# The second network's first matrix product as seven Strassen block products, with its weight blocks streamed from DRAM scratch

## The chip, the cores and the metric

The kernel runs on one core of a Trainium2 chip. The metric is the device time of one launch in microseconds; three runs of the kernel before took 911.65, 911.95 and 911.99 us, median 911.95 us.

## What is computed

Attention over a window of 128 positions, then two dense networks one behind the other, over 2304 tokens of width 512, hidden width 2048:

```python
x = attention(q, k, v)                  # (2304, 512)
h = np.maximum(x @ w_in, 0.0)
x = h * h @ w_out                       # first network, "layer 0"
h = x @ w2_in                           # (2304, 512) @ (512, 2048)
g = h * np.cos(h)
out = g @ w2_out                        # second network, "layer 1"
```

All is float32. Each matrix product is made of three: both operands are split into a high part, rounded to the multiplier's format, and the low rest; high by high, high by low and low by high are added in PSUM.

## The kernel before

**Units.** `ORDER` (lines 44 to 52) lists 144 units of work. A unit is one block of tokens and one column block f of 128 hidden columns (16 of them): `h_mms(i)` makes the hidden values (4 contraction tiles x 3 matmuls, L584 to L586, into one PSUM bank), an element-wise stage follows, and `y_mms(i)` multiplies with the second matrix into four PSUM banks that collect over all f (4 output tiles x 3 matmuls, L661 to L663). Blocks 0 to 3 have 512 tokens; block 4 has 256 and takes two f in a unit. Units 0 to 71 are layer 0 (48 to 71 alternate two units of block 3 and one of block 4), 72 to 135 layer 1 on blocks 0 to 3, and 136 to 143 layer 1 on block 4.

**Element-wise stage.** Layer 0: `relu_part` and `square_part` (relu and high part on ACT, square and low part on DVE). Layer 1: `cos_reduce` (ACT `kk`, two DVE steps, a DVE clamp, ACT abs) and `cos_apply` (ACT sine, DVE product with h, ACT high part `gh`, DVE low part `gl`). h stays in PSUM until the product.

**Order.** Per unit the loop at L825 emits `cos_apply` of the next unit, one `tick`, the h products of the unit `LA` ahead (L833: 1, later 2, then 3), the element-wise stage, another `tick`, and the two halves of `y_mms`. ACT, DVE, POOL and SP run in the order that the scheduler gives them, each strictly in turn. `tick` moves the prepared jobs by one stage: weights (`w_job`: a load of 1 MB for each f and layer, `w_top` on ACT, `w_rest` on DVE, high part on ACT, low part on DVE) and layer 1's input (`x2_job`: high part on ACT, low part on DVE). A weight of layer 1 takes the place of the layer-0 weight of the same f in SBUF and can be loaded when the last unit that reads it is done. So all sixteen f of layer 1 lie in SBUF, ready for the multiplier.

**PSUM.** Four banks collect y; four (`h_slot`) take h of layer 1 in turn.

Of the kernel before, what the change touches and what calls it, by code (L numbers as in the profile page):

```python
# [22 lines left out]
P = 128  # L23
NJ = NT // P
T = 256
# [39 lines left out]


ENGINES = {mybir.EngineType.PE, mybir.EngineType.Activation, mybir.EngineType.DVE, mybir.EngineType.Pool}


class Job:  # L70


    def __init__(self, key, load, stages, gates=None, source=None, frees=1, ready=None):
        self.key, self.load, self.stages, self.frees = key, load, stages, frees
        self.gates, self.source, self.ready = gates or {}, source, ready
        self.raw, self.at = None, 0


@with_exitstack
def attention_mlp_mlp(ctx: ExitStack, tc: tile.TileContext, kq, s0, v, w1, w2, bias, ident, out):  # L80
# [37 lines left out]

    W, A2, Y = {}, {}, {}
    QH, QL, V = {}, {}, {}  # L120
    now = {"qk": -1, "v": -1, "h": -1, "y": -1}

    queues = {"a": [], "w": []}
    inflight, finished = [], set()
# [5 lines left out]
    def top_up():  # L132
        for c in "aw":
            if c == "a" and now["qk"] < A_OPEN:
                continue
            jobs = queues[c]
            while held[c] < AHEAD[c] and loads[c] < len(jobs):
                job = jobs[loads[c]]
                if job.source is not None and job.source not in finished or job.ready and not job.ready():
                    break  # L140
                job.queue = c
                if c == "a":
                    job.raw = rp.tile([P, 512], F32, tag=c, name=f"raw_{c}{loads[c]}")
                job.load(job)
                held[c] += 1
                loads[c] += 1

    def advance(job):
        job.stages[job.at](job)
        if job.at == job.frees:  # L150
            held[job.queue] -= 1
# [6 lines left out]
    late = []  # L158

    def tick(new="aw", flush=True):  # L160
        for job in list(inflight):
            if job.at not in job.gates or job.gates[job.at]():
                if not advance(job):
                    inflight.remove(job)
        while late and flush:
            late.pop(0)()
        top_up()
        for c in new:
            if started[c] < len(queues[c]):
                job = queues[c][started[c]]  # L170
                if job.raw is not None and (0 not in job.gates or job.gates[0]()):
# [23 lines left out]

    def clear(key):
        t = cv.tile([P, 1024], F32, tag="cv", name="cv_" + "_".join(map(str, key)))
        pool.memset(t, 0.0)
        return t

    def w_top(job):

        job.t = cleared.pop(0) if cleared else clear(job.key)
        top = job.t.bitcast(F16).rearrange("p (n two) -> p n two", two=2)
        act.copy(top[:, :, 1], job.raw.bitcast(BF16).rearrange("p (n q) -> p n q", q=4)[:, :, 2])
# [12 lines left out]
    def w_split(job):  # L220
        _, layer, f = job.key
        w = W[layer, f] = wp.tile([P, 2048], F32R, tag=f"w{f}", name=f"w_{layer}_{f}")
        act.copy(w[:, 0:1024], job.t)

        def lo():
            dve.tensor_tensor(w[:, 1024:2048], job.t, w[:, 0:1024].bitcast(F32), ALU.subtract)  # L226

        late.append(lo)

    def w_job(layer, f):  # L230

        last = max((i for i, (a, _, fs, _) in enumerate(ORDER) if a == layer - 1 and f in fs), default=-1)
        seen = 4 * min(f - SEAT + 1, PLAIN - 1) + 3

        def ready():
            if layer == 0 and f >= SEAT:
                return now["qk"] >= seen and now["v"] >= START - 1
            return now["y"] >= last

        return Job(("w", layer, f), w_load(layer, f), [w_top, w_rest, w_split], frees=2, ready=ready)  # L240


# [6 lines left out]
    def x_ready(layer, b):  # L249
# [3 lines left out]
        return now["h"] >= max((i for i, unit in enumerate(ORDER) if unit[:2] in old), default=-1)  # L253

    def x2_job(b, m):
        def view(part):
            x = XS[x_slot(1, b)][part]
            return x[:, :, m, :] if b < NBK else x[:, 0, 2 * m : 2 * m + 2, :]

# [306 lines left out]
    def h_mms(i):  # L566
        layer, b, fs, n = ORDER[i]
        if layer == 1:
            for m in range(KT if b < NBK else 2):
                run_until(("x", b, m))  # L570
        for f in fs:
            run_until(("w", layer, f))
        now["h"] = i
        hpool, tag = h_slot(i)
        hb = hpool.tile([P, 2, T], F32, tag=tag, name=f"h_{i}")
        Hb[i] = hb
        for c, f in enumerate(fs):
            wh, wl = W[layer, f][:, 0:512], W[layer, f][:, 1024:1536]
            o = hb[:, c] if len(fs) == 2 else hb
            for kt in range(KT):  # L580
                cs = slice(kt * P, kt * P + P)
                xs = XS[x_slot(layer, b)]
                xh, xl = (part[:, :, kt] if n is None else part[:, n, kt] for part in xs)
                te.matmul(o, wh[:, cs], xh, start=(c == 0 and kt == 0), stop=False, skip_group_check=True)  # L584
                te.matmul(o, wh[:, cs], xl, start=False, stop=False, skip_group_check=True)  # L585
                te.matmul(o, wl[:, cs], xh, start=False, stop=(kt == KT - 1), skip_group_check=True)  # L586

# [4 lines left out]
    def square_part(i):  # L592
# [9 lines left out]
        lo = dve.tensor_tensor(rl, a, rh.bitcast(F32), ALU.subtract)  # L602
        A2[i] = (rh, rl)
        return hi, lo

# [11 lines left out]
    def cos_apply(i):  # L617
# [5 lines left out]
        dve.tensor_tensor(r, r, hb, ALU.mult)  # L623
        act.copy(rh, r)  # L624
        dve.tensor_tensor(rl, r, rh.bitcast(F32), ALU.subtract)  # L625
        A2[i] = (rh, rl)
# [6 lines left out]
    def y_mms(i, cs, ms=range(KT)):  # L633
# [11 lines left out]
        if tokens_out(layer, b):  # L645
            for t in ms if tuple(ms) != tuple(range(KT)) else range(2):
                for c in cs:
                    wh, wl = (W[layer, fs[c]][:, k : k + 512] for k in (512, 1536))
                    gh, gl = (g[:, c, t * P : t * P + P] for g in (rh, rl))
# [5 lines left out]
        for m in ms:  # L655
            o = Y[b][m // 2][:, m % 2] if two else Y[b][m] if n is None else Y[b][m][:, n]
            for c in cs:
                wh, wl = (W[layer, fs[c]][:, k + m * P : k + m * P + P] for k in (512, 1536))
                gh, gl = (rh[:, c], rl[:, c]) if per == 2 else (rh, rl)
# [10 lines left out]
    def y_out(layer, b):  # L670
        for k, yb in enumerate(Y.pop(b)):
            if gp2 is not None and k % 2:
                ysb = gp2.tile([P, 2, T], F32, tag="ysb", name=f"ysb_{layer}_{b}_{k}")
            else:
                ysb = gp.tile([P, 2, T], F32, tag="a", name=f"ysb_{layer}_{b}_{k}")
            (dve.tensor_copy if k % 2 else act.copy)(ysb, yb)  # L676
# [8 lines left out]
    def y_tail(i):  # L685

        for t in range(2):
            y_mms(i, (0, 1), (t,))
            for k, copy in enumerate((dve.tensor_copy, act.copy)):
                ypool, tag = (gp, "a") if t else (gp2, "ysb")  # L690
                ysb = ypool.tile([P, 2, T], F32, tag=tag, name=f"ysb_tail_{t}_{k}")[:, 0]
                copy(ysb, Y[NBK][t][:, k * T : k * T + T])
# [3 lines left out]


    MARKS = [(-1, START), (14, 32), (29, 50), (30, 52), (45, 66), (48, STEPS)]

# [6 lines left out]
    for j in range(PLAIN - 1, NJ):  # L706
        queues["a"] += [kq_job(j, hp) for hp in range(4)]
    queues["a"] += [x2_job(b, m) for b in range(NBK + 1) for m in range(KT if b < NBK else 2)]
    queues["w"] += [w_job(layer, f) for layer in range(2) for f in range(NF)]

    with ExitStack():
# [113 lines left out]
        for i in range(len(ORDER)):  # L825
            if s >= STEPS and gp2 is None:
# [5 lines left out]
                gp2 = ctx.enter_context(tc.tile_pool(name="gp2", bufs=2))  # L832
            LA = 1 if i < NG1 - 2 else 2 if i < NG1 else 3  # L833
# [5 lines left out]
            if i + 1 < len(ORDER) and ORDER[i + 1][0] == 1:  # L839
                cos_apply(i + 1)  # L840
            tick("aw" if s >= STEPS else "a")
            new = range(emitted, min(i + LA + 1, len(ORDER)))
            emitted = max(emitted, new.stop)
            for m in new:
# [11 lines left out]
            if i + 1 == len(ORDER):  # L856
                y_tail(i)
                break
            if len(ORDER[i][2]) == 2:
# [3 lines left out]
            y_mms(i, *halves[0])  # L863
            if todo > 0:
                values_of_block()
                s += 1
            if todo > 1:
# [3 lines left out]
                s += 1  # L871
            y_mms(i, *halves[1])
            values_of_block()

# [60 lines left out]
```

## Time and profile before

| | |
|---|---|
| runs | 911.65, 911.95, 911.99 us |
| profiled execution | 911.92 us, its span 910.1 us, granted clock 0.997 |
| PE busy | 900.4 us, 99% of the span |
| DVE, ACT, POOL busy | 582.9, 473.5, 93.1 us |
| DMA | 69.18 MB, mean 76 GB/s |

The span runs from the first to the last instruction; 1.8 us lie around it. A matmul's duration in the records overlaps the next one's, so its cost is the distance between two starts. In a timeline row the first number is the start, the second the duration, and the bracket at its end says how long the engine was idle before and what ended that.

### The profile page before, as it was taken

How to read it: one execution, taken by the hardware profiler on the slowest of the kernel's cores; microseconds unless marked ns; L12 is line 12 of the kernel's file. 1: busy time of each engine (PE TensorE's matmuls, PEld its weight loads, DVE VectorE, ACT ScalarE, POOL GpSimd, SP SyncE). 2: the span in 40 equal slices, each digit the busy share in tenths (PEclk: the TensorE clock that was granted, in tenths of full speed). 3: DMA queues.
4: the chain of work that ended last, by engine and by line, in shares of the span. 5: the costliest groups of instructions: out<-in, count | busy, mean ns of one | idle time of the engine just before them, and what ended most of it. 6: DMA issues, size and time to landing. Idle time of an engine off the chain costs nothing.

```text
span 910.1 us, 13087 instructions
## 1 busy us (share of the span) xinstructions
PE 900.4 (99%) x4898; PEld 748.2 (82%) x4898; DVE 582.9 (64%) x1343; ACT 473.5 (52%) x1018; POOL 93.1 (10%) x164
## 2 busy tenths in 40 slices
PE   9899999999999999999999999999999999999998
PEld 7677788788888888888888888888888888888897
DVE  7699676666676666745454785665566555655553
ACT  6799555454454444544454774454444444444443
POOL 3332221101111111201011000000000000000000
PEclk9999999999999999999999999999999999999999
DMA  9752032311121111242423620020001000100010
GB/s 369 284 223 94 13 127 70 102 50 59 47 90 61 59 47 47 83 139 98 179 94 125 212 103 1 13 81 1 0 1 47 1 1 0 47 1 1 1 47 23
DMA packets 25870, 69.18 MB, mean 76 GB/s; under 512 B 2640, under 2 KB 8144, under 8 KB 25808
## 3 DMA queue, kind: packets, MB, share of 16 engines
q1 hardware_dynamic: 25376, 68.16, 21.3%
q8 instruction: 38, 0.62, 0.3%
q10 hardware_dynamic: 432, 0.20, 0.1%
q14 instruction: 24, 0.20, 0.1%
HBM read 58.91 MB, written 9.44 MB: 75 GB/s over the span
## 4 chain that ended last, share of the span: by engine, by line
PE 88%; DVE 7%; ACT 3%; issue 1%; DMA 1%; POOL 0%; DVEq 0%; ACTq 0%; POOLq 0%
PE h L584 13%; PE h L585 13%; PE h L586 13%; PE y L661 13%; PE y L663 12%; PE y L662 12%; PE o L532 3%; PE s L380 2%; PE t L479 1%; DVE cv_w L211 1%; DVE w L226 1%; PE junk L114 1%; PE y L651 1%; PE y L652 1%; PE y L653 1%
## 5 line engine op out<-in xcount | busy, mean ns | idle before, releaser
L584 PE MATMUL h<-xh,w 128*128 128x512 f32 (+1 forms) x640 | 237.3, 371 | 0.0
L585 PE MATMUL h<-xl,w 128*128 128x512 f32 (+1 forms) x640 | 236.1, 369 | 0.0
L586 PE MATMUL h<-xh,w 128*128 128x512 f32 (+1 forms) x640 | 235.8, 368 | 0.0
L584 PEld LDWEIGHTS h<-xh,w 128*128 128x128 f32 x640 | 120.7, 189 | 21.0 <-issue 0.3
L586 PEld LDWEIGHTS h<-xh,w 128*128 128x128 f32 x640 | 120.6, 189 | 20.5
L585 PEld LDWEIGHTS h<-xl,w 128*128 128x128 f32 x640 | 120.8, 189 | 18.8
L661 PE MATMUL y<-rh,w 128*128 128x512 f32 (+1 forms) x320 | 123.2, 387 | 0.5 <-DVE ysb L676 0.5
L663 PE MATMUL y<-rh,w 128*128 128x512 f32 (+1 forms) x320 | 118.5, 370 | 0.0
L662 PE MATMUL y<-rl,w 128*128 128x512 f32 (+1 forms) x320 | 118.4, 370 | 0.0
L614 ACT ACTIVATE r<-r 128x512 f32<-128x512 f32 x72 | 45.5, 632 | 120.1 <-DVE r L613 120.1
L661 PE MATMUL y<-gh,w 128*128 128x512 f32 x256 | 99.6, 390 | 0.2 <-ACT gh L624 0.2
L662 PE MATMUL y<-gl,w 128*128 128x512 f32 x256 | 99.6, 389 | 0.0
L663 PE MATMUL y<-gh,w 128*128 128x512 f32 x256 | 99.6, 389 | 0.0
L625 DVE TENSOR_TENSOR gl<-r,gh 128x512 fp32r<-128x512 f32 x72 | 49.8, 691 | 74.2 <-ACT gh L624 74.1
L611 DVE SCALAR_TENSOR_TENSOR r<-kk,h 128x512 f32<-128x512 int32 x72 | 49.5, 687 | 63.9 <-ACT kk L610 63.8
L601 DVE TENSOR_TENSOR a<-a 128x512 f32<-128x512 f32 x62 | 44.3, 715 | 59.1 <-ACT rh L600 56.4
L610 ACT ACTIVATE kk<-h 128x512 int32<-128x512 f32 x72 | 43.0, 597 | 69.7 <-PE h L586 69.6
L590 ACT ACTIVATE a<-h 128x512 f32<-128x512 f32 x72 | 42.9, 596 | 69.0 <-PE h L586 67.4
L446 ACT ACTIVATE p<-s,st 128x128 f32<-128x128 f32 x112 | 40.1, 363 | 68.7 <-DVE st L430 64.3
L486 POOL TENSOR_SCALAR_AFFINE_SELECT p<-p 128x256 f32<-128x256 f32 x104 | 50.2, 483 | 246.2 <-ACT p L481 235.9
L663 PEld LDWEIGHTS y<-rh,w 128*128 128x128 f32 x320 | 60.3, 189 | 10.7
L661 PEld LDWEIGHTS y<-rh,w 128*128 128x128 f32 x320 | 60.3, 189 | 10.5 <-issue 1.7
(91 smaller groups left out, 1398.2 us busy)
## 6 DMA issues: line engine op xcount, KB each, us to landing
raw<-w_in SPq DMA_DIRECT2D x32, 1023.8 KB, 6.8
raw_a<-kq_in SPq DMA_DIRECT2D x44, 256.0 KB, 2.5
v<-v_in SPq DMA_DIRECT2D x18, 256.0 KB, 2.7
y<-ysb SPq DMA_DIRECT2D x18, 256.0 KB, 2.1
raw_a<-y SPq DMA_DIRECT2D x18, 256.0 KB, 2.8
out<-ysb SPq DMA_DIRECT2D x16, 256.0 KB, 2.3
s<-s_in SPq DMA_DIRECT2D x6, 512.0 KB, 9.4
s<-s_in SPq DMA_DIRECT2D x2, 256.0 KB, 3.2
```

Of the source, the lines that this page charges most:

```text
L486: pool.affine_select(pt[:, part], pt[:, part if quick else 0], pattern=[[0, n], [0, 2], [-sign, P]], compare_op=ALU.is_gt if part else ALU ...
L584: te.matmul(o, wh[:, cs], xh, start=(c == 0 and kt == 0), stop=False, skip_group_check=True)
L585: te.matmul(o, wh[:, cs], xl, start=False, stop=False, skip_group_check=True)
L586: te.matmul(o, wl[:, cs], xh, start=False, stop=(kt == KT - 1), skip_group_check=True)
L601: dve.tensor_tensor(a, a, a, ALU.mult)
L610: act.activation(kk, hb, AF.Copy, scale=INV2PI)
L611: dve.scalar_tensor_tensor(r, kk, -C1, hb, ALU.mult, ALU.add)
L614: act.activation(r, r, AF.Abs)
L625: dve.tensor_tensor(rl, r, rh.bitcast(F32), ALU.subtract)
L661: te.matmul(o, wh, gh, start=(first and not (two and m % 2)), stop=False, skip_group_check=True)
L662: te.matmul(o, wh, gl, start=False, stop=False, skip_group_check=True)
L663: te.matmul(o, wl, gh, start=False, stop=last, skip_group_check=True)
```

## The change

For blocks 0 to 3 of layer 1, two units (one pair u of column blocks, 256 hidden columns) become one group p = 8 b + u. Its matrix product is cut in 2 x 2 blocks of 256 and made by Winograd's form of Strassen's scheme: seven block products where the plain product has eight. `seven(p, part)` has 7 x 2 contraction tiles x 3 = 42 matmuls of 256 columns; before, two units had 24 of 512. Three products open PSUM regions d, z and e; z takes four of the seven products in turn. After each of them a copy or an addition moves what it holds to a tile of h in SBUF: per group four ACT copies and three DVE additions of 128x256. `seven` runs two groups ahead of y, in four parts, one before each half of `y_mms`. `cos_reduce` and `cos_apply` read h from SBUF.

Weights: for each u, `blocks_job` turns the first matrices of two f into the blocks A11 to A22 and their sums S1 to S4, splits these in high and low parts, and stores all eight (2 MB) in DRAM scratch `wd[u]`; `w2_job` prepares the second matrices in place. The SBUF that this frees is the arena: 20 places of 256 KB in a ring, in which `stream()` loads the seven blocks of each group (four for block 4), and tiles 0, 1 and 7 for blocks of the input. `x2_sums_job` makes the input's sums T1 to T4. A job's stage waits `LEAD` = 5 ticks behind the load; `behind()` puts these stages behind the latest element-wise operation of ACT and DVE, and stores are issued one stage after the work that fills them. `y_out` takes all its buffers from one pool of two (before: two pools).

```diff
+BLOCKS = ("A11", "A12", "A21", "A22", "S1", "S2", "S3", "S4")
+SEVEN = (("A12", "B21"), ("A11", "B11"), ("S1", "T1"), ("S2", "T2"), ("S3", "T3"), ("S4", "B22"), ("A22", "T4"))
+RING = range(2, NU - 1)
...
+    def blocks_job(u):
...
+        def sums(job):
...
+            dve.tensor_tensor(s1, a21, a22, ALU.add)
+            dve.tensor_tensor(s3, a11, a21, ALU.subtract)
+            dve.tensor_tensor(s2, s1, a11, ALU.subtract)
+            dve.tensor_tensor(s4, a12, s2, ALU.subtract)
+            hi(job, 0)
+        def middle(job):
+            lo(job, 0)
+            hi(job, 1)
+        def more(job):
+            lo(job, 1)
+            store(job, 0)
+        def end(job):
+            store(job, 1)
...
+    def stream():
+        while streamed[0] < len(groups):
...
+            if now["p"] < g - 2 or ticks[0] < landed.get(u, 1 << 30) or any(a not in Arena for a, _ in places):
+                return
+            for (a, c), name in zip(places, names):
+                Chunk[g, name] = Arena[a][:, 512 * c : 512 * c + 512]
+                sp.dma_start(Chunk[g, name].bitcast(F32), wd[u][:, BLOCKS.index(name)])
...
+    def seven(p, part):
...
+            places = ((ps_y2, "z0"), (ps_y2, "z1")) if p % 2 else ((ps_h, "h"), (ps_h2, "h"))
...
+        d, z, e = one[:, 0], one[:, 1], two[:, 0]
...
+        if part == 0:
+            product(0, d, opens=True)
+            product(1, z)
+            product(2, e, opens=True)
+            act.copy(h1[:, 0], z)
+            act.copy(h2[:, 1], e)
+            dve.tensor_tensor(h1[:, 0], h1[:, 0], d, ALU.add)
+        elif part == 1:
+            product(3, z)
+            act.copy(h1[:, 1], z)
+        elif part == 2:
+            product(4, z)
+            dve.tensor_tensor(h2[:, 1], h2[:, 1], z, ALU.add)
+        else:
+            product(5, e)
+            dve.tensor_tensor(h1[:, 1], h1[:, 1], e, ALU.add)
+            product(6, z)
+            act.copy(h2[:, 0], z)
...
+            if i >= NG1 and i < L0:
+                p, c = divmod(i - NG1, 2)
+                for q in (2 * c, 2 * c + 1):
+                    tick()
+                    if q == 0:
+                        cos_apply(i + 1)
...
+                    if p + 2 < NP:
+                        seven(p + 2, q)
...
+                    y_mms(i, (0,), (0, 1) if q % 2 == 0 else (2, 3))
...
+            if i == NG1 - 2:
+                seven(0, 0)
+                seven(0, 1)
             y_mms(i, *halves[0])
```

The instructions' order, at three places (names: h or hs hidden values in PSUM or SBUF, s the PSUM regions of a group, numbered by group; r, gh, gl by unit; the last number is a buffer's).

ACT, layer 1, before: one unit.

```order
L610 ACTIVATE kk_117_7167<-h_117_7154 128x512
L614 ACTIVATE r_117_7168<-r_117_7168 128x512
L624 CAST gh_116_7186<-r_116_7130 128x512
L622 ACTIVATE r_117_7168<-r_117_7168,halfpi_81 128x512
```

ACT, layer 1, now: one group (two units).

```order
L855 COPY hs_24_0_8302<-s_24_0_8300 128x256
L901 ACTIVATE r_118_8294<-r_118_8294 128x512
L856 COPY hs_24_1_8303<-s_24_1_8301 128x256
L909 ACTIVATE r_118_8294<-r_118_8294,halfpi_81 128x512
L901 ACTIVATE r_119_8332<-r_119_8332 128x512
L909 ACTIVATE r_119_8332<-r_119_8332,halfpi_81 128x512
L860 COPY hs_24_0_8302<-s_24_0_8300 128x256
L911 CAST gh_118_8351<-r_118_8294 128x512
L897 ACTIVATE kk_120_8403<-hs_24_0_8302 128x512
L868 COPY hs_24_1_8303<-s_24_0_8300 128x256
L897 ACTIVATE kk_121_8441<-hs_24_1_8303 128x512
L911 CAST gh_119_8397<-r_119_8332 128x512
```

The four copies stand between the steps of the units of the group before; the third (L860), which frees z for the fifth product, stands behind the sines of both units.

ACT around the start of layer 1, now (cv and hi_b belong to `blocks_job` and `w2_job` of u = 6):

```order
L283 CAST w_1_6_5649<-cv_w2_6_5605 128x1024
L855 COPY hs_1_0_5610<-s_1_0_5608 128x256
L901 ACTIVATE r_72_5554<-r_72_5554 128x512
L909 ACT_TABLE_LOAD
L909 ACTIVATE r_72_5554<-r_72_5554,halfpi_81 128x512
L901 ACTIVATE r_73_5591<-r_73_5591 128x512
L856 COPY hs_1_1_5611<-s_1_1_5609 128x256
L860 COPY hs_1_0_5610<-s_1_0_5608 128x256
L336 CAST hi_b_6_5598<-s_b_6_5633 128x1024
L911 CAST gh_72_5651<-r_72_5554 128x512
```

The copies of group 1 that free e (L856) and z (L860) now stand behind the first units' reduction and the table load.

DVE a little later, now (`cv_p` and `s_b` low parts of the blocks of u = 6, `w_1_6` of its second matrices):

```order
L912 TENSOR_TENSOR gl_72_5652<-r_72_5554,gh_72_5651 128x512
L340 TENSOR_TENSOR s_b_6_5633<-s_b_6_5633,hi_b_6_5598 128x1024
L290 TENSOR_TENSOR w_1_6_5649<-cv_w2_6_5605,w_1_6_5649 128x1024
L910 TENSOR_TENSOR r_73_5591<-r_73_5591,hs_0_1_5464 128x512
L898 SCALAR_TENSOR_TENSOR r_74_5706<-kk_74_5705,hs_1_0_5610 128x512
L857 TENSOR_TENSOR hs_2_0_5714<-hs_2_0_5714,s_2_0_5712 128x256
L912 TENSOR_TENSOR gl_73_5700<-r_73_5591,gh_73_5699 128x512
L899 SCALAR_TENSOR_TENSOR r_74_5706<-kk_74_5705,r_74_5706 128x512
L898 SCALAR_TENSOR_TENSOR r_75_5751<-kk_75_5750,hs_1_1_5611 128x512
L900 TENSOR_SCALAR r_74_5706<-r_74_5706 128x512
L899 SCALAR_TENSOR_TENSOR r_75_5751<-kk_75_5750,r_75_5751 128x512
L240 SCALAR_TENSOR_TENSOR cv_p_7_5747<-raw_b_7_5599,cv_p_7_5747 128x1024
```

Two 1024-wide low halves now stand ahead of unit 73's product (L910), and a 1024-wide step of u = 7 follows among unit 75's.

## Rows read from the trace of the kernel before

**Rows 1.** The page, part 1: busy time, share and instructions of each engine.

```profile
PE 900.4 (99%) x4898; PEld 748.2 (82%) x4898; DVE 582.9 (64%) x1343; ACT 473.5 (52%) x1018; POOL 93.1 (10%) x164
```

**Rows 2.** Windows: stretch, its length, busy time by engine, clock, DMA share, GB/s.

```profile
450.00:500.00 50.00, 50.00 (x289) 44.23 (x289) 26.37 (x30) 24.56 (x30) 5.74 (x6) 1.00 0.35 127
510.00:515.00 5.00, 5.00 (x23) 4.13 (x22) 5.00 (x9) 3.54 (x8) 0.96 (x1) 1.00 0.51 177
515.00:520.00 5.00, 4.78 (x32) 4.17 (x31) 3.97 (x7) 4.45 (x7) 0.00 (x0) 1.00 0.97 319
600.00:650.00 50.00, 50.00 (x222) 41.40 (x221) 29.35 (x48) 23.18 (x39) 0.00 (x0) 1.00 0.06 22
```

**Rows 3.** Timeline of PE: starts of 512-column, then 256-column matmuls in layer 1.

```profile
600.02 0.39 PE L661 MATMUL y<-gh,w 128*128 128x512 f32 x1
...
602.74 0.39 PE L584 MATMUL h<-xh,w 128*128 128x512 f32 x1
...
869.84 0.28 PE L584 MATMUL h<-xh,w 128*128 128x256 f32 x1
...
872.72 0.40 PE L651 MATMUL y<-w,gh 128*128 128x512 f32 x1
```

**Rows 4.** Groups by line: one matmul line at 256 columns, and its weight loads.

```profile
L584 PE MATMUL h<-xh,w 128*128 128x256 f32 x128 | 36.1, 282 | 0.0
L584 PEld LDWEIGHTS h<-xh,w 128*128 128x128 f32 x640 | 120.7, 189 | 21.0 <-issue 0.3
```

**Rows 5.** Groups of DVE by line and shape: busy us, mean ns of one, idle before.

```profile
L211 DVE SCALAR_TENSOR_TENSOR cv_w<-raw,cv_w 128x1024 int32<-128x1024 int32 x30 | 36.6, 1223 | 0.9 <-ACT cv_w L207 0.5
L611 DVE SCALAR_TENSOR_TENSOR r<-kk,h 128x512 f32<-128x512 int32 x72 | 49.5, 687 | 63.9 <-ACT kk L610 63.8
L613 DVE TENSOR_SCALAR r<-r 128x512 f32<-128x512 f32 x72 | 30.7, 426 | 2.1
L312 DVE TENSOR_TENSOR ql<-raw_a,qh 128x256 fp32r<-128x256 f32 x44 | 18.6, 423 | 1.3 <-PE s L380 1.2
```

**Rows 6.** Groups of ACT by line and shape.

```profile
L622 ACT ACTIVATE r<-r,halfpi 128x512 f32<-128x512 f32 x72 | 51.9, 721 | 0.3
L207 ACT CAST cv_w<-raw 128x1024 f16<-128x1024 bf16 x30 | 41.1, 1371 | 2.2 <-DMA raw<-w_in 1.4 <-POOL cv_w L198 0.8
L622 ACT ACT_TABLE_LOAD x1 | 1.3, 1283 | 0.0
L692 ACT COPY ysb_tail<-y 128x256 f32<-128x256 f32 x2 | 0.7, 372 | 5.1 <-DVE ysb_tail L692 5.1
```

**Rows 7.** Timeline of ACT and of DVE in one unit of layer 1.

```profile
600.22 0.60 ACT L610 ACTIVATE kk<-h 128x512 int32<-128x512 f32 x1 [1.13 <-PE h L586]
...
603.30 0.60 ACT L624 CAST gh<-r 128x512 fp32r<-128x512 f32 x1
603.81 0.72 ACT L622 ACTIVATE r<-r,halfpi 128x512 f32<-128x512 f32 x1
...
600.85 0.69 DVE L611 SCALAR_TENSOR_TENSOR r<-kk,h 128x512 f32<-128x512 int32 x1 [1.05 <-ACT kk L610]
601.58 0.69 DVE L612 SCALAR_TENSOR_TENSOR r<-kk,r 128x512 f32<-128x512 int32 x1
...
603.94 0.69 DVE L625 TENSOR_TENSOR gl<-r,gh 128x512 fp32r<-128x512 f32 x1 [1.21 <-ACT gh L624]
604.56 0.69 DVE L623 TENSOR_TENSOR r<-r,h 128x512 f32<-128x512 f32 x1
```

**Rows 8.** Timeline of PE at a pause, and the window behind it (clock before the DMA share).

```profile
32.99 0.62 PE L479 MATMUL t<-id_sb,s 128*128 128x128 f32 x3 [1.18 <-ACT s L468]
...
34.00:38.00 4.00, 4.00 (x32) 2.72 (x28) 1.20 (x3) 1.85 (x3) 2.40 (x3) 0.57 0.93 379
```

**Rows 9.** The page, part 6: DMA issues, KB each, median us from issue to landing.

```profile
raw<-w_in SPq DMA_DIRECT2D x32, 1023.8 KB, 6.8
raw_a<-y SPq DMA_DIRECT2D x18, 256.0 KB, 2.8
```

More of the change, by code (lines that the diff above doesn't have):

```diff
@@ L136, in top_up @@
             jobs = queues[c]
-            while held[c] < AHEAD[c] and loads[c] < len(jobs):
+            while loads[c] < len(jobs) and held[c] + jobs[loads[c]].raws <= AHEAD[c]:
                 job = jobs[loads[c]]
@@ L142, in top_up @@
                 if c == "a":
-                    job.raw = rp.tile([P, 512], F32, tag=c, name=f"raw_{c}{loads[c]}")
+                    raws = [rp.tile([P, 512], F32, tag=c, name=f"raw_{c}{loads[c]}_{r}") for r in range(job.raws)]
+                    job.raw = raws[0] if job.raws == 1 else raws
                 job.load(job)
-                held[c] += 1
+                job.loaded = ticks[0]
+                held[c] += job.raws
                 loads[c] += 1
+        stream()
     def advance(job):
-        job.stages[job.at](job)
+        with behind() if job.key[0] in ("p", "w2") else ExitStack():
+            job.stages[job.at](job)
         if job.at == job.frees:
-            held[job.queue] -= 1
+            held[job.queue] -= job.raws
         job.at += 1
@@ L158, in attention_mlp_mlp, with behind @@
     late = []
+    ticks = [0]
+    latest = {}
+    def behind(*engines):
+        back = ExitStack()
+        for e in engines or ("act", "dve"):
+            if e in latest:
+                back.enter_context(tc.issue_after(latest[e].ins))
+        return back
     def tick(new="aw", flush=True):
+        ticks[0] += 1
         for job in list(inflight):
@@ L170, in tick @@
                 job = queues[c][started[c]]
-                if job.raw is not None and (0 not in job.gates or job.gates[0]()):
+                if job.raw is None or job.key[0] in ("p", "w2") and ticks[0] < job.loaded + LEAD:
+                    continue
+                if 0 not in job.gates or job.gates[0]():
                     started[c] += 1
@@ L244, in attention_mlp_mlp, with run_stream @@
+    def run_stream(g):
+        for _ in range(400):
+            if streamed[0] > g:
+                return
+            tick()
+        raise RuntimeError(f"group {g}")
     XS = [[xp.tile([P, 2, KT, T], F32R, name=f"x{part}_{i}") for part in "hl"] for i in range(2)]
@@ L567, in h_mms @@
         layer, b, fs, n = ORDER[i]
+        g = NP + fs[0] // 2
         if layer == 1:
-            for m in range(KT if b < NBK else 2):
+            for m in range(2):
                 run_until(("x", b, m))
-        for f in fs:
-            run_until(("w", layer, f))
+            run_stream(g)
+            now["p"] = g
+        else:
+            for f in fs:
+                run_until(("w", layer, f))
         now["h"] = i
@@ L671, in y_out @@
         for k, yb in enumerate(Y.pop(b)):
[L672 to L675, printed above, removed]
+            ysb = gp.tile([P, 2, T], F32, tag="a", name=f"ysb_{layer}_{b}_{k}")
             (dve.tensor_copy if k % 2 else act.copy)(ysb, yb)
@@ L872, in attention_mlp_mlp @@
             y_mms(i, *halves[1])
+            if i == NG1 - 1:
+                cos_reduce(NG1 + 1)
+                for q in range(4):
+                    tick()
+                    if q == 2:
+                        cos_apply(NG1)
+                    seven(1, q)
             values_of_block()
```

259 lines of the change are left out of this document (226 added, 33 removed).

## The prediction

> **What bounds the kernel now.** The page's busy times come first: PE works 99% of the span, DVE 64%, ACT 52% [rows 1]. The windows then tell where the rest is: in the stages that the change touches PE is full in every stretch (50.00 of 50 us in layer 1) and loses 0.22 us at the one change of stage, where DVE is busy for a whole 5 us [rows 2]. So the time is PE's issue time, and what PE costs is read from distances between starts: twelve matmuls of 512 columns take 602.74 - 600.02 = 2.72 us, 226.7 ns each; twenty-four of 256 columns take 872.72 - 869.84 = 2.88 us, 120.0 ns each [rows 3]. The records of a 256-column matmul (282 ns) and of its weight load (189 ns) are longer [rows 4], but overlap.
>
> **What PE gains.** A pair of units in layer 1 has 24 h matmuls, 24 x 226.7 = 5.44 us. A group has 42 of 256 columns, 42 x 120.0 = 5.04 us. That is 0.40 us for each of 32 groups, **12.8 us**: not an eighth of the 174 us of these products, because half the columns cost 53% of the time. The Trainium skill (TensorE: Matmul & The Clock Gate, "Wait — 56ns, not 53.3ns?") gives a warm matmul its columns at 2.4 GHz and only about 2.5 ns besides; by that a group would save 24 x 215.8 - 42 x 109.2 = 593 ns, all groups 19.0 us, and the sum below would be 902.7. The rows contradict it here: both widths show some 13 ns beside their columns, so the halved width costs, and the sum goes by the rows. Layer 0 and block 4 keep their matmuls.
>
> **What a group adds beside PE.** Four copies of 128x256 on ACT (372 ns in the nearest row [rows 6]) and three additions on DVE (423 ns [rows 5]). Taken as throughput both fit: a pair of units (10.88 us) has 5.0 us of ACT and 6.4 of DVE now (23.18 and 29.35 of 50 us [rows 2]), and 1.5 and 1.3 come in, for 10.48 us. What counts is the chain, since z must be emptied before the next product may write it. I schedule one group by hand. Spacings [rows 7]: on DVE a dependent step starts 0.73 after the one it needs (601.58 - 600.85), an independent one 0.62 (604.56 - 603.94), at a record of 0.69; a hand-over to another engine takes 0.03 (600.85 - 600.22 - 0.60). So I let independent steps overlap by 0.07 to 0.09.
> Zero is a group's first product. Three products end at 2.16, half a y (6 x 226.7 = 1.36) at 3.52, S2 at 4.24, y at 5.60, S3 at 6.32, y at 7.68, S4 and A22 at 9.12, y at 10.48. S4's last result is there at 8.56; DVE's addition hands h to ACT's `kk` at 9.05; then DVE, in its order, starts the first unit's reduction 9.68, its second step 10.41, the other unit's first 11.02, the older unit's low half 11.64, a clamp 12.26, an addition 12.62, the other unit's second step 12.98, its clamp 13.71. ACT's abs follows at 14.17, the sine (721 ns [rows 6]) at 14.83, and behind it, at 15.46, the copy that frees z after S2: done 15.83. PE wants z at 10.48 + 5.60 = 16.08. **It fits by 0.25 us**, so I take 10.48 us for a group and no wait. The bounds: nothing, or, with every step at its full record (0.1 us more at six places, 0.6 in all), a wait of 0.35 us in every one of the 26 groups behind the start-up.
> At a block's end four copies of y come in. With two buffers instead of four the third waits for the first one's store, but y's banks are wanted 3.5 us or more after they close; nothing taken. The input's sums (2.2 us of ACT, 4.2 of DVE, twice per block) stand, for blocks 2 and 3, where the chain has gaps; nothing taken.
>
> **The joint stage** (units 48 to 71) has ACT and DVE half busy [rows 2]. A pair of column blocks, 16.6 us of PE, gets 1.2 us more of ACT and 2.9 of DVE (one more split and four sums), so DVE comes to about 73%. Between a unit's h and its own y lie 5.4 us of other products and the relu chain needs 2.0; the longest stretch put between (4.2 us on DVE) leaves room. Nothing; if that cover went, each wait would be 1 us or so.
>
> **The start of layer 1** is where it costs. Before, up to three units of h waited in PSUM; now groups 1 and 2 need z and e emptied while the blocks of u = 6 and 7 are still being made. Zero is the end of y of unit 68. Without waits PE would end group 0 and y of unit 70 at 16.1, y of 71 at 19.0, group 1 with two products of group 2 at 25.4.
> (a) From 13.7 on DVE has no gap: additions of group 0, copies of y, a 1024-wide merge (1223 ns [rows 5]) for each half of u = 6, sums, the reductions of units 72 and 73. Unit 72's clamp ends near 21.8, and ACT then has abs, the table load (1283 ns), sine and the other abs [rows 6] ahead of the copy of e, which starts at 25.0. S4 of group 1 waits until 25.4, and PE ends that stretch at 27.8: **2.4 us**.
> (b) Two 1024-wide low halves stand ahead of unit 73's product; `gh_73` ends at 31.5, PE wanted it at 30.5: **1.0**.
> (c) Two ACT tops for u = 7 (1371 ns each [rows 6]) and a merge stand ahead of unit 74's; `gh_74` ends at 37.4, PE has had nothing since 35.0: **2.4**.
> (d) In groups 3 to 5 the sums of block 1 stand between: three waits of 0.2 to 0.3 for z, and 1.8 at `gh_78`, behind a run of six copies and low parts: **2.5**.
> Together **8.3 us**. Bounds: 0.2 (what the change of stage loses now) and, if none of these steps overlaps, about 12.
> DMA: a group's seven blocks are 1.84 MB per 10.48 us, 175 GB/s, where a window of 319 is full [rows 2]. They are issued a group ahead and a 256 KB load lands in 2.8 us [rows 9]; nothing. The stores of u = 6 leave by 29.4, and group 2's third block, loaded behind them, is there by 34, wanted at 38.
>
> **The clock.** After PE waited 1.18 us for ACT, on top of smaller pauses, four microseconds ran at a granted 0.57, most of them at 1.2 GHz, a loss of 0.43 x 4 = 1.7 us [rows 8]. Pauses (a) and (c) are longer. I count 1.7 for each, and half of it hidden, since (b) and (d) wait for DVE and ACT anyway: 1.7, rounded to **1.5 us** (ends 0 and 3.4).
>
> **Sum.** 911.92 (the profiled execution, 0.03 below the median) - 12.8 + 8.3 + 1.5 = **908.9 us**.
>
> **The rivals.**
> *Start-up hidden.* DVE and ACT keep up, and the start costs 2 to 4 us and no clock: 901 to 904, taken as 902. For it: now PE loses 0.22 us there with DVE full [rows 2]. Against: the order puts e's copy behind the table load, and that h has to leave PSUM first. 0.20.
> *The z chain is longer than a group* (slower). Place: ACT's copy after S2, PE's S3. It decides as soon as the chain from S4's result to that copy exceeds 7.5 us; each 0.1 us above gives 2.6 us over 26 groups. With full records 0.35 x 26 = 9.1, so 918; from 0.2 us a group on it is slower than before. For it: a margin of 0.25 in a chain of twelve steps on two engines that take turns. Against: the measured overlaps. 0.20.
> *The ring is late.* A load takes the 6.8 us of a 1 MB one [rows 9] where SP holds it back behind block 1's input (group 5's blocks can go only at 57.7, wanted from 62.4 on): 2 to 5 us, 911 to 914. 0.10, half of it within 0.2% of before.
> *The narrow products don't gain:* weight loads bind at their 189 ns. Then a group is 42 x 0.189 + 5.44 = 13.4 us, and the kernel 80 us slower. Against: the 24 matmuls of 120.0 ns each have a load of their own [rows 3, 4]. 0.02.
>
> **How the numbers follow.** My case, 905 to 912.5, has 0.48: of that 0.33 is more than 0.2% (1.8 us, about what a measurement of this kernel tells from no change) below 911.95, 0.15 within it. Faster: 0.33 + 0.20 = 0.53. Same: 0.15 + 0.05 = 0.20. Slower: 0.20 + 0.05 + 0.02 = 0.27. The likeliest time is 908.9; the range, 901 to 918, takes in the hidden start-up and the long chain at full records, and leaves out the narrow products, start-up costs beyond the bound, and a still longer chain.
>
> **What would show it.** Right: in layer 1's later part (groups 8 to 31) PE busy throughout, 42 matmuls of 256 columns at 120 ns, about 10.48 us a group; PE's idle rows released by ACT's copy of e and by `gh` in the first 50 us of layer 1, 7 to 10 us in all; a clock below 1 in those stretches alone. Wrong: idle time before S3 in every group, released by ACT (the long chain); PE waiting for DMA (the ring); under 4 us of waits at the start (hidden).

## The result, and the profile after

The changed kernel takes **917.18 us** (median of four runs, 915.92 to 918.14) against 911.95: 1.0057 times as long, interval 1.004 to 1.0075. The forecast was 908.9, faster. The time lies in the range, the sign is wrong. The profiled execution took 917.38 us, 5.46 more than that of before (911.92).

Page, part 1, of the changed kernel (before: [rows 1]):

```profile
PE 895.1 (98%) x5474; PEld 764.6 (84%) x5474; DVE 647.7 (71%) x1533; ACT 533.6 (58%) x1176; POOL 93.9 (10%) x164
```

PE has 5.3 us less to do and yet ends later: 20.5 us of its span of 915.6 are idle, 9.7 before. Where, the windows tell (before: [rows 2]; stretch, its length, busy time of PE, PEld, DVE, ACT, POOL, then clock, DMA share, GB/s):

```profile
450.00:500.00 50.00, 49.84 (x287) 43.90 (x287) 37.00 (x56) 29.66 (x41) 4.72 (x5) 1.00 0.90 304
510.00:515.00 5.00, 5.00 (x32) 4.20 (x32) 4.90 (x8) 1.57 (x4) 0.41 (x1) 1.00 1.06 382
515.00:520.00 5.00, 3.96 (x34) 3.76 (x32) 3.02 (x6) 4.42 (x6) 1.44 (x2) 1.00 0.85 274
520.00:525.00 5.00, 3.46 (x26) 3.26 (x27) 5.00 (x10) 3.62 (x7) 0.00 (x0) 1.00 0.99 274
535.00:540.00 5.00, 2.31 (x12) 1.65 (x12) 3.44 (x7) 2.81 (x5) 0.95 (x1) 1.00 0.82 267
540.00:545.00 5.00, 4.22 (x22) 3.83 (x20) 4.26 (x8) 3.29 (x7) 0.00 (x0) 0.66 0.97 297
600.00:650.00 50.00, 48.83 (x304) 43.46 (x303) 38.63 (x75) 32.00 (x64) 0.00 (x0) 1.00 0.68 208
```

The joint stage holds (49.84 of 50). The idle time lies from 515 to 545, and a little at the ends of blocks (48.83 of 50 in the window that holds the first of three). What was not in the forecast stands in the last two columns: the DMA engines are nearly full well before layer 1, 304 GB/s where it was 127. In part 6, the loads of layer 1's matrices (two pairs of 512 KB for each u, all issued between 397 and 526 us):

```profile
arena<-wd SPq DMA_DIRECT2D x256, 256.0 KB, 3.2
raw<-w_in SPq DMA_DIRECT2D x16, 511.8 KB, 7.3
raw_b<-w_in SPq DMA_DIRECT2D x16, 511.8 KB, 7.0
```

In the trace of before the sixteen loads of the same matrices, 1 MB each, landed in 6.3 us (median): half the size, in runs of up to four, now takes longer. The 6.8 us of [rows 9] are a median over these and layer 0's early loads.

PE's waits from 490 us on (line, releaser: us in total, times, longest):

```profile
PE s L847 <- DMA arena<-wd: 2.7, 1, 2.7
PE s L847 <- ACT ysb L960: 2.5, 1, 2.5
PE y L948 <- ACT gh L911: 1.9, 3, 0.8
PE s L847 <- DVE hs L857: 1.7, 4, 0.7
PE s L847 <- ACT hs L856: 1.2, 1, 1.2
```

Two of the five I had not costed: a ring block that is late, and the copy of layer 0's y (`ysb`), which frees the bank that group 1 opens as z. On the timeline of PE:

```profile
518.68 0.28 PE L950 MATMUL y<-rh,w 128*128 128x256 f32 x1
521.41 0.39 PE L847 MATMUL s<-arena,arena 128*128 128x256 f32 x1 [2.45 <-ACT ysb L960]
...
536.58 0.39 PE L950 MATMUL y<-gh,w 128*128 128x512 f32 x1
539.65 0.39 PE L847 MATMUL s<-arena,arena 128*128 128x256 f32 x1 [2.69 <-DMA arena<-wd]
...
541.41 0.79 PE L948 MATMUL y<-gh,w 128*128 128x512 f32 x1 [0.78 <-ACT gh L911]
542.00 0.41 PE L847 MATMUL s<-xh,arena 128*128 128x256 f32 x1
542.21 0.41 PE L848 MATMUL s<-xl,arena 128*128 128x256 f32 x1
```

Behind the second pause the spacing of narrow matmuls is 0.21 instead of 0.12: eleven of them at the lower clock, 1.2 GHz (542.00 to 544.35), 1.0 us.

The steady group is whole, but longer than forecast. A group on the same timeline: y (512 columns), one narrow product, y again:

```profile
666.47 0.40 PE L948 MATMUL y<-gh,w 128*128 128x512 f32 x1
...
667.85 0.28 PE L847 MATMUL s<-xh,arena 128*128 128x256 f32 x1
...
668.57 0.40 PE L948 MATMUL y<-gh,w 128*128 128x512 f32 x1
```

Six narrow matmuls take 0.72 us, 120.0 ns each, as forecast. Six wide ones take 1.38 (mean of 29 halves 1.385), not 1.36. Four halves make the group 10.56 us, not 10.48.

Last, the end of a block. PE, DVE and SP:

```profile
625.52 0.38 PE L847 MATMUL s<-xh,arena 128*128 128x256 f32 x1 [0.73 <-DVE hs L857]
```

```profile
623.85 0.69 DVE L960 COPY ysb<-y 128x512 f32<-128x512 f32 x1 [0.67 <-DMA out<-ysb]
624.46 0.68 DVE L912 TENSOR_TENSOR gl<-r,gh 128x512 fp32r<-128x512 f32 x1
625.06 0.41 DVE L857 TENSOR_TENSOR hs<-hs,s 128x256 f32<-128x256 f32 x1
```

```profile
619.45 0.42 SPq L400 DMA_DIRECT2D arena<-wd  x1
619.96 0.41 SPq L965 DMA_DIRECT2D out<-ysb  x1
```

The second copy of y on DVE has no buffer until the store of DVE's first copy lands. That store was issued at 619.96, in turn with ring loads, and landed at 623.76, 3.8 us later. Behind the waiting copy stands the addition that frees d, which PE needs.

**Where the 5.46 us are.** Executions of one kernel differ by some 3 us (that of before: 908.8 to 912.0), most of it early: two profiles that run the same instructions up to there (e5 and e7 below) reach one matmul of the joint stage at 372.76 and 370.04. So I compare profiles from the start of group 0's first product to PE's last matmul. Counting that stretch's 1560 matmuls of 256 columns at 120.0 ns and 876 of 512 at 226.7 gives 385.8 us; the changed kernel took 404.0. Of the 18.2: steady groups 32 x 0.08 = 2.6; ends of blocks 3.4 (from ACT's copy L855 of group 6 to that of group 31: 267.38 against 25 x 10.56 = 264.00); the rest, some 12.5, is the start of layer 1 (72.12 us to L855 of group 6, for 288 narrow and 108 wide matmuls, 59.0 us, and half a microsecond of the 0.08 each). Another 0.9 is lost before (the end of unit 68's y, 499.34 against 498.48), less than executions differ there.

### The profile page after: what moved, and what is told of

It reads as the page before. It is cut to its first block, busy times and chain, and to the rows that moved or that the text cites. A ratio compares the mean times of both kernels' runs of the same rounds, so it can differ in the third digit from the quotient of the medians.

```text
span 915.6 us, 15361 instructions
## 1 busy us (share of the span) xinstructions
PE 895.1 (98%) x5474; PEld 764.6 (84%) x5474; DVE 647.7 (71%) x1533; ACT 533.6 (58%) x1176; POOL 93.9 (10%) x164
## 4 chain that ended last, share of the span: by engine, by line
PE 70%; DVE 15%; DMA 6%; ACT 5%; issue 2%; POOL 1%; SPq 0%; POOLq 0%; DVEq 0%; ACTq 0%
PE y L948 10%; PE y L949 10%; PE y L950 10%; PE h L819 6%; PE h L820 6%; PE h L821 6%; PE s L847 4%; PE s L849 4%; PE s L848 4%; PE o L760 2%; DMA raw_a<-y 2%; PE s L608 2%; DVE cv_w L240 1%; DMA raw_a<-kq_in 1%; PE t L707 1%
## 5 line engine op out<-in xcount | busy, mean ns | idle before, releaser
L819 PE MATMUL h<-xh,w 128*128 128x512 f32 (+1 forms) x320 | 119.7, 374 | 0.0
L820 PE MATMUL h<-xl,w 128*128 128x512 f32 (+1 forms) x320 | 118.4, 370 | 0.0
L821 PE MATMUL h<-xh,w 128*128 128x512 f32 (+1 forms) x320 | 118.1, 369 | 0.0
L847 PE MATMUL s<-xh,arena 128*128 128x256 f32 x256 | 73.8, 288 | 2.3 <-DVE hs L857 1.7
L848 PE MATMUL s<-xl,arena 128*128 128x256 f32 x256 | 72.8, 285 | 0.0
L849 PE MATMUL s<-xh,arena 128*128 128x256 f32 x256 | 72.7, 284 | 0.0
L897 ACT ACTIVATE kk<-hs 128x512 int32<-128x512 f32 x64 | 40.3, 633 | 55.5 <-DVE hs L866 54.7
L819 PEld LDWEIGHTS h<-xh,w 128*128 128x128 f32 x320 | 60.5, 189 | 10.6 <-issue 0.3
L821 PEld LDWEIGHTS h<-xh,w 128*128 128x128 f32 x320 | 60.3, 189 | 10.5
L949 PEld LDWEIGHTS y<-rl,w 128*128 128x128 f32 x320 | 60.6, 189 | 8.4 <-DVE rl L887 0.5
```

The lines of the kernel that those rows point to most:

```text
L819: te.matmul(o, wh, xh, start=(c == 0 and kt == 0), stop=False, skip_group_check=True)
L820: te.matmul(o, wh, xl, start=False, stop=False, skip_group_check=True)
L821: te.matmul(o, wl, xh, start=False, stop=(kt == KT - 1), skip_group_check=True)
L847: te.matmul(o, wh, xh, start=opens and k == 0, stop=False, skip_group_check=True)
L848: te.matmul(o, wh, xl, start=False, stop=False, skip_group_check=True)
L849: te.matmul(o, wl, xh, start=False, stop=k == 1, skip_group_check=True)
```

## The experiments

The numbers behind each run: the whole time as a ratio to the kernel before on the same chip, and from the profile (a) group 0's first product to PE's last matmul, (b) to ACT's copy L855 of group 6, (c) from there to that of group 31 (264.00 without waits).

| run | ratio | a | b | c |
|---|---|---|---|---|
| changed kernel, first chip | 1.0057 (1.004 to 1.0075) | 404.04 | 72.12 | 267.38 |
| e5_again | 1.0047 (1.0032 to 1.0062) | 400.67 | 70.24 | 265.89 |
| e1_memset | 1.0045 (1.0031 to 1.0059) | 400.63 | 70.41 | 265.68 |
| e6_y0 | 1.0041 (1.0024 to 1.0057) | 400.92 | 69.93 | 266.45 |
| e2_ring16 | 1.0020 (1.0003 to 1.0037) | 399.48 | 69.58 | 265.36 |
| e3_ring16_y4 | 1.0010 (0.9997 to 1.0023) | 399.32 | 69.74 | 265.04 |
| e4_noload | 1.0019 (1.0006 to 1.0031) | 399.36 | 70.82 | 264.00 |
| e7_both | 0.9982 (0.9969 to 0.9994) | 395.60 | 66.78 | 264.28 |
| e8_both_later | 0.9997 (0.9981 to 1.0012) | 398.25 | 63.71 | 269.99 |
| e9_later_1_2 | 0.9997 (0.9986 to 1.0007) | 396.44 | 65.85 | 266.05 |
| e10_later_1_3 | 0.9960 (0.9943 to 0.9977) | 396.62 | 67.74 | 264.34 |
| e14_hold_7 | **0.9940 (0.9922 to 0.9958)** | 394.44 | 63.71 | 266.19 |

**e5_again: the changed kernel as it is.** 

> The changed kernel itself, on the chip of the next three, so that they stand beside it and not beside another chip's runs. Both theories: 1.0057 of the kernel before, as measured (1.004 to 1.0075), some 5 us more, with single runs that lie up to 3 us apart, since the transfers of the start fall differently.

 As expected; its profile sets the scale: between two profiles of one program (a) differs by 3.4 us, 1.9 of it at the start and 1.5 at the block ends.

**e1_memset.** On ACT's timeline of the changed kernel the top of u = 6 waits 3.11 us for a memset, and that for the store of u = 5's tile; the copy `ysb` comes behind. The chain of releasers there (start, us, what):

```profile
508.90 5.58 DMA wd<-cv_p
514.59 0.96 POOL cv_p L226
515.58 1.38 ACT cv_p L236
```

```diff
-            if u in (0, 2, 4):
+            if u in (0, 2, 4, 5):
```

> Only the place of one tile changes: the zeroed tile of u = 5's blocks lies in the buffer that u = 0, 2 and 4 use, so that the memset for u = 6 no longer waits for the store of u = 5. Theory (late transfers hold buffers, and through the memset ACT's queue): ACT's 3.1 us of idle time at 512.5 to 515.6 goes, the copy of block 4's y comes about 2 us earlier, PE's 2.5 us in front of group 1 shrink to under 1, and the kernel takes 914 to 915.5 against 917.2. Rival (ACT and DVE are themselves too busy there; the memset only fills time that the queue lacks anyway): within 0.5 us of 917.2, and PE waits as long a little later.

 The wait for the memset went, and nothing else: PE still waits 2.7 us for `ysb`. The rival has the time right but not the reason. On ACT, in e1_memset:

```profile
521.26 0.59 ACT L960 COPY ysb<-y 128x512 f32<-128x512 f32 x1 [0.80 <-DMA y<-ysb]
```

The copy itself waits for a store, issued at 517.00 and landed at 521.19, 4.2 us (median of these stores in the kernel before: 2.1): six copies of y share two buffers. Two causes stood one behind the other.

**e2_ring16.**

```diff
-RING = range(2, NU - 1)
+RING = range(2, NU - 2)
```

> The ring has 16 places instead of 20 (a group's loads are issued two groups ahead, so 14 places are enough), and no load waits until the blocks of u = 6 are stored. Theory (the ring is late by that order): PE's 2.7 us of waiting for the first block of group 3 go, 914 to 916. Rival (the transfers themselves are slow because the DMA engines are full then): PE still waits 1.5 us or more for a load in groups 2 to 4, 916.5 to 917.5.

 The wait for the ring falls from 2.7 (1.4 in e5_again) to 0.4. But (b) falls by only 0.7 us against e5_again: that PE waited there hid other work that was late. The interval of the ratio touches that of e5_again, so the size of this gain alone isn't settled.

**e6_y0.** As e1_memset, and:

```diff
+        early = layer == 0 and b >= NBK - 1
+        if early:
+            spare = xp.tile([P, KT, 2, T], F32, tag=f"x{part}_1", name=f"ysb_0_{b}")
...
+            if early:
+                ysb = spare[:, k]
```

> As the run with the other place for u = 5's tile, and besides the last six copies of layer 0's y (blocks 3 and 4) get a buffer each, in the input tile of block 3, which nothing reads by then. Theory (PE waits 2.5 us for z because the copy of block 4's y has no free buffer until an earlier store lands): with both causes gone PE's wait for that copy falls from 2.7 us to under 0.7, and the time is 2 to 4 us below the changed kernel's. Rival (ACT's own queue of tops and parts of u = 6 delays it): PE still waits 2 us or more there.

 Right on the mechanism, not on the time. PE's waits in e6_y0:

```profile
PE s L847 <- DMA arena<-wd: 3.0, 1, 3.0
...
PE s L847 <- ACT ysb L967: 0.5, 1, 0.5
```

PE's wait for z falls from 2.7 to 0.5 us, but (b) by 0.3 alone: PE comes to the ring earlier and waits there, 3.0 us.

**e7_both: e1, e2, e6 and four buffers for layer 1's y (as e3) together.** 

> All repairs so far together: the ring of 16 places, the other place for u = 5's tile, a buffer for each copy of y from block 3 of layer 0 on. Theory (three separate delays by buffers and transfers: z 2.7, ring 2.7, block ends 3 to 4): 8 us below the changed kernel, about 909 where the kernel before takes 911.4. Rival (what is freed in one place is waited for in the next): 912 or more, with DVE and ACT (copies behind the tops and low parts of u = 6 and 7) as the releasers.

 Here the gains come: (b) 66.8, 3.5 us below e5_again, where the ring alone gave 0.7 and the buffers alone 0.3; (a) 5.1 less. Theory and time agree (909.27 us), though the gain on the changed kernel of the same chip is 5.8, not 8. This version is faster than both kernels.

**e3_ring16_y4.** As e2, and:

```diff
+            if layer == 1:
+                ysb = Arena[6][:, 512 * k : 512 * k + 512].bitcast(F32).rearrange("p (n t) -> p n t", n=2)
+            else:
                 ysb = gp.tile([P, 2, T], F32, tag="a", name=f"ysb_{layer}_{b}_{k}")
```

> As the ring of 16, and the tile that this frees holds four buffers for layer 1's y, one for each bank, where the change has two. Theory (two buffers cost about 1 us at each end of a block, since the third copy waits for the first store and DVE stands behind it): the long groups at the block ends (11.0 to 11.5 us) come down to 10.6, about 3 to 4 us less than with the ring alone. Rival (they are long for the copies' own time on ACT and DVE, or for the input's sums): less than 1 us.

 Against e2 alone (c) falls by 0.3 us, as the rival said. The stretch (c) also holds other waits: e8, e9 and e14 have four buffers and lose 6.0, 2.0 and 2.2 us in it, most or all of it by group 15. From L855 of group 15 to that of group 31, which holds the last two block ends, the kernels with two buffers and the ring's loads lose 0.65 (e2) to 1.7 us, those with four 0 to 0.2, e9 0.66. So the buffers explain most of it, and one profile each is too few for the size.

**e4_noload.**

```diff
+                if g < 8:
                     sp.dma_start(Chunk[g, name].bitcast(F32), wd[u][:, BLOCKS.index(name)])
```

> From group 8 on the ring's blocks are not loaded again: the products of blocks 1 to 3 read what lies there (their results are other numbers). Theory (in the steady groups PE's 512-column matmuls take 230.5 ns instead of 226.7 because they run between narrow ones, whatever the DMA does): 10.56 us a group as before, within 1 us of 917.2. Rival (the ring's 175 GB/s disturb PE's reads or delay ACT and DVE): 10.48 us a group, 2 us less, and the block ends shorter.

 Two answers. Every group takes 10.56 us still, with the DMA at 25 GB/s from 664 to 686 (193 with the loads): the 0.08 us are not the ring's. And (c) is 264.00, no loss at any block end, with two buffers: the copies wait only because of the ring's loads. The twelve stores of y for blocks 0 to 2 land in 2.4 to 4.5 us in the changed kernel (median 3.6) and in 2.1 to 2.9 here (median 2.1). Whether a store is late by the traffic or by its place behind loads in the queue, this run does not tell apart.

**e13_narrow_h: what lengthens a wide product?** The kernel before, with

```diff
+                if layer == 1 and n is None:
+                    for t in range(2):
+                        te.matmul(o[:, t], wh[:, cs], xh[:, t], start=(kt == 0 and t == 0), stop=False, skip_group_check=True)
...
+                    continue
```

> The kernel before with each 512-column product of layer 1's hidden values cut into two of 256 columns; its y products and all else stay. Theory (512-column products take 230.8 ns, not 226.7, where they run between narrow ones): a pair of units takes 48 x 120.0 ns + 24 x 230.8 ns = 11.30 us, 0.42 us more than 10.88, 13.4 us over 32 pairs, and the halves of y (six products) measure 1.385 us. Rival (the 1.385 us come from something else in the changed kernel, such as DVE and ACT being busier or the places of the operands): 11.20 us a pair, 10.2 us more in all, halves of y at 1.36.

 923.98 us, ratio 1.0136 (1.0117 to 1.0155). A unit takes 5.62 us, a pair 11.24, between the two. The timeline of PE in this run, y's twelve products of one unit:

```profile
704.98 0.40 PE L667 MATMUL y<-gh,w 128*128 128x512 f32 x1
...
706.37 0.39 PE L667 MATMUL y<-gh,w 128*128 128x512 f32 x1
...
707.73 0.28 PE L586 MATMUL h<-xh,w 128*128 128x256 f32 x1
```

The first six, behind narrow ones, take 1.39 us, the next six 1.36. So it is not every wide product (my theory's form) but a cost of some 0.025 us each time PE goes from 256 to 512 columns. A group has four such places, a unit here one. Why, no run here shows.

**e8_both_later, e9_later_1_2, e10_later_1_3: u = 6 and 7 later.** On top of e7, the first stage of the two jobs waits for a group (2 and 4; 1 and 2; 1 and 3):

```diff
-        return lambda: u < NU - 1 or now["p"] >= 1
+        return lambda: u < NU - 2 or now["p"] >= 2 * (u - NU) + 6
```

> As the run before, and the work on u = 6 and u = 7 (tops, sums, parts, stores) is begun two and four groups later, when groups 2 and 4 are made. Theory (what then remains at the start of layer 1 is ACT's and DVE's work on these two u, in front of the copies and of gh_73 and gh_74): 3 to 5 us less than without it, and PE's waits for gh and for the copies of e and z in groups 1 to 4 under 1 us in all. Rival (a group's own chain is what is late there): within 1 us of it.

 The first half came true: (b) is 63.7, 3.1 below e7. Then (c) gives 5.7 back; PE's waits in e8_both_later:

```profile
PE y L948 <- ACT gh L911: 3.0, 3, 1.6
PE s L847 <- DMA arena<-wd: 1.2, 1, 1.2
```

All three waits for gh lie between 587 and 615 us: block 1's input needs a place that u = 7's blocks leave, and its sums, parts and the work on u = 7 now fall on the same groups.

> As the run with all repairs, and the work on u = 6 and u = 7 begins when groups 1 and 2 are made (not 2 and 4). Theory (the first groups wait for ACT and DVE because of this work, and block 1's input, which needs u = 7's place, was late where it began at 2 and 4): from the first product of group 0 to that of group 6 some 62 to 64 us (65.2 with all repairs, 61.2 with 2 and 4), no wait at 590 to 625, 2 to 4 us less than with all repairs alone, ratio 0.994 to 0.997. Rival (the work costs its time wherever it stands): within 1 us of 0.998.

 A miss: (b) is 0.9 below e7, (c) gives 1.8 back, and the time is no better. The waits for gh (2.2 us in three, the longest 1.4) have moved to 543, 563 and 574.

> The same with 1 and 3. Theory: the first seven groups as with 1 and 2, u = 7 half a block before block 1 begins; if block 1's input is then late, up to 3 us of waits at 590 to 625 as with 2 and 4. Rival: within 1 us of 0.998 as well.

 The ratio is better than e9's, and the intervals do not overlap, but (a) is no better (396.6 and 396.4): in these two profiles what differs lies ahead of group 0 (504.9 and 508.1 us), where neither edit acts and executions differ anyway. So which spacing is best isn't settled. The waits for gh are down to 0.7 us; what stands out is one wait for the ring, 1.9 us.

**e14_hold_7.** As e10, and the two loads of u = 7 wait for group 1:

```diff
-            ready=lambda: now["y"] >= used(u) and gp2 is not None,
+            ready=lambda: now["y"] >= used(u) and gp2 is not None and (u < NU - 1 or now["p"] >= 1),
```

> As the run with u = 6 and u = 7 begun at groups 1 and 3, and u = 7's two loads (2 MB) are issued once group 1 is made, so that group 2's blocks stand ahead of them in SP's queue. Theory (what is left of PE's waiting for a load, 1.9 us in group 2, is the queue's order): that wait under 0.5 us, 1 to 3 us less from the first product of group 0 to the end (396.6 us), ratio 0.993 to 0.996. Rival (the DMA engines are full there, whatever comes first): still 1 us or more for a load, within 1 us of 396.6.

 PE's waits in e14_hold_7:

```profile
PE y L948 <- ACT gh L911: 1.7, 2, 0.9
PE s L847 <- DVE hs L863: 1.4, 1, 1.4
PE s L847 <- DMA arena<-wd: 0.3, 2, 0.2
```

The wait for the ring is down to 0.3 in two pieces, (a) 2.2 us shorter, as the theory said (4.0 less in (b), 1.9 more in (c)). In e10 the block of group 2's first product is issued at 519.77, right behind u = 7's loads, and lands 9.0 us later; here it goes ahead of them, at 517.17, and lands in 3.8. The DMA engines are nearly full both times (shares of 0.93 and 0.96 from 520 to 525): with full engines the order in SP's queue decides which load is late. 905.69 us, the lowest time found, 0.6% below the kernel before, though the interval overlaps e10's; (b) has come from 70.2 to 63.7.

**e11_no_tie and e12_lead_1: two parts of the change undone.**

```diff
-        for e in engines or ("act", "dve"):
+        for e in engines:
```

> The changed kernel without the tie that puts the stages of the two weight jobs behind the latest rectifier or sine step of ACT and DVE (stores stay behind the loads before them). Theory (the joint stage has room on both engines, and the loss lies in layer 1): 0 to 3 us more than the changed kernel, from waits of about 1 us for the first network's high and low parts between 300 and 500 us. Rival (the tie itself makes the tops and copies late at the start of layer 1): 2 us less or better.

 936.35 us, ratio 1.0281 (1.0263 to 1.0298): 21 us more than e5_again (on another chip; the ratios give the same), far beyond the theory's 3. Group 0 begins at 525.4 instead of 507.9, so 17.5 of it is lost before layer 1. PE's waits from 300 us on begin with

```profile
PE y L949 <- DVE rl L887: 11.3, 6, 2.7
```

the first network's low part, which stands behind weight work on DVE: in the longest of these waits DVE is at the weights from 486.44 on, but for one step, and begins the low part at 492.72.

```diff
-    LEAD = 5
+    LEAD = 1
```

> The changed kernel with one half step between a weight's load and its first stage instead of five. Theory (a load takes 7 to 8 us in the joint stage, a half step some 4, so a top would stand in ACT's order before its data are there, and the rectifier behind it): 3 to 12 us more, PE waiting for ACT and DVE between 390 and 500 us. Rival (loads land well ahead in any case, since two more are under way): within 1 us of the changed kernel.

 922.34 us, ratio 1.0117 (1.0102 to 1.0132): 7.3 more than e5_again, as the theory said; in the profiles group 0 begins 8.9 later, and (a) is 399.81, 0.9 less. ACT's own waits in e12_lead_1, 372 to 510 us:

```profile
ACT cv_p L236 <- DMA raw_b<-w_in: 19.8, 5, 6.3
```

The top stands in ACT's order before its load has landed, up to 6.3 us, and the rectifier behind it.

## Why the prediction was wrong, step by step

**PE's gain: mis-sized, 10.2 us and not 12.8.** The narrow products cost 120.0 ns as read. The y products were taken over at 226.7 ns, unchanged; each half behind narrow ones costs 0.02 to 0.025 us more, 0.08 a group, 2.6 us in all. The estimate from the Trainium skill's figure (TensorE: Matmul & The Clock Gate, "Wait — 56ns, not 53.3ns?"), 19.0 us, would have been further off. The trace of before held the answer six matmuls behind the last row I read [rows 3]: in block 4, y's first six products, behind narrow ones, start at 872.72, the next six at

```profile
874.10 0.39 PE L651 MATMUL y<-w,gh 128*128 128x512 f32 x1
```

and the next narrow one at 875.46: 1.38, then 1.36 us.

**The steady group: no wait, as forecast.** No gap in any group away from the block ends. ACT's copy behind S2, the tightest link, in the group that begins at 674.87:

```profile
679.33 0.37 ACT L860 COPY hs<-s 128x256 f32<-128x256 f32 x1
```

It ends at 679.70, and PE takes z at 680.51: a margin of 0.8, where I had 0.25. The rival of the long chain (0.20) falls.

**Block ends: "nothing taken", and 1.4 to 3.4 us were lost.** I asked when PE wants y's banks (late enough) and not what stands behind the waiting copy on DVE: the additions that free z, e and d. Nor did I ask how long a store takes among the ring's loads: 3.6 us in the middle, 2.1 without them (e4_noload).

**The joint stage: nearly right.** 0.9 us by the end of unit 68, within what executions differ by then. e11 and e12 show that it is the tie and the lead that make it so.

**The start of layer 1: 9.8 forecast with the clock, some 12.5 measured, and made of other things.** From the distances between starts on PE's timeline, less 120.0 or 226.7 ns: (a) the copy of e and what follows it, 1.9 us (forecast 2.4); (b) gh_73, 1.1 (1.0); (c) gh_74, 1.3 (2.4); (d) groups 3 to 5, 0.6 (2.5); the clock 1.0 (1.5). With 0.8 in two short waits (at 509.4 and 524.7) these sum to 6.7, less than the 9.8 that were forecast.

The step that failed is *"DMA: ... nothing"*, and with it the order in which I read the start: 2.8 us for a ring block and 2.6 for z, neither in the sum. I divided a group's bytes by its time (175 GB/s) in the steady state, and did not add the joint stage's 4 MB for each u (2 MB loaded, as before, and 2 MB stored) to the ring's loads. The stores of u = 6 were to leave by 29.4 and group 2's third block to be there by 34; they left by 32.2 (531.54), and behind them group 3's first block, which PE wanted at 37.6, landed at 40.3 (539.61) and group 2's third at 41.6 (540.94). With the DMA at a share of 1.04 and 1.06 from 505 to 515 us, u = 5's store took 5.6 us, the memset waited for its buffer, and the copy that frees z stood behind that on ACT; with the memset out of the way (e1_memset) the copy waited for another store. And SP, which issues in order, held group 3's blocks behind u = 6's stores and u = 7's loads. The rival of the late ring (0.10, 2 to 5 us) had the mechanism, at group 5 instead of group 3.

**The sum.** -12.8 + 2.6 + 12.5 + 3.4 + 0.9 = 6.6; the kernel before itself loses 0.7 us in the same stretch by the same count, which leaves 5.9, against 5.46 measured. Against the forecast the miss is 3.4 at the block ends, 2.7 at the start, 2.6 in the wide products and 0.9 ahead, less those 0.7. The start is that near only because two errors offset each other: 5.4 us of DMA left out, and some 3 us too much for the steps that were priced. That the time lies in the range is luck too: the range's upper end came from the long chain, which did not occur. The narrow products stood, and the clock's cost by its size, though it fell after the wait for the ring and not after (a) or (c).

The delays are not additive: e2 and e6 each removed one of the two waits and gained 0.7 and 0.3 at the start; together they gained 3.5 (in e7, whose buffers for layer 1's y act only behind (b)). That the DMA is nearly full in the joint stage was seen but no run took bytes away there, so what it costs by itself stays open.

## What to carry to other kernels

When a change adds DMA traffic, cost it stage by stage against what already runs in that stage, and follow each store to the buffer it holds, the copy that wants the buffer, and what stands behind that copy on its engine. In a queue that issues in order, a load that waits for its place holds all that follow: a ring with no more places than its look-ahead needs, and loads that can wait put behind those that cannot, took away most of the waits for the ring here (e2, e14) with all the bytes still moved. Where a stretch has two waits in a row, take away both before judging either.

## What the runs showed of the hardware

- Going from 256-column to 512-column matmuls costs 0.02 to 0.03 us each time (1.38 to 1.39 us for the first six, 1.36 for the next), with or without DMA traffic.
- The granted clock fell to its lower level after PE pauses of 2.69 us (0.66 in the five microseconds from 540) and 1.85 us (e10). It did not after one of 2.45 us in the changed kernel nor after one of 2.81 us in e2, at the same place where 2.75 us (e5) and 2.65 us (e1) were followed by it. So a pause's length alone does not tell.
- Among the ring's loads (193 GB/s in a steady stretch) a 256 KB store of y lands in 2.4 to 4.5 us, without them (25 GB/s) in 2.1 to 2.9. A 256 KB load issued right behind 2 MB of other loads landed 9.0 us later, one issued ahead of them 3.8 us (e10, e14).
- A DMA share above 1.00 is shown at 382 GB/s.
